# fp16 high and low halves for the later bounds, weight transfers each held behind keys, and constant rows written later, in a chunk-selecting attention with a feed-forward block

## The chip, the core and the metric

The kernel runs on one core of one Trainium2 chip. The metric is the device time of one execution in microseconds (us), lower is better. The core has a matrix engine (TensorE, PE in the profile; its weight loads are listed as PEld), a vector engine (VectorE, DVE), an activation engine (ScalarE, ACT), a general engine (GpSimd, POOL) and a queue engine (SyncE, SP) that here only starts transfers. Each works through its own list of instructions in order; semaphores tie them together.

## What is computed

Attention on 4 images x 8 heads x 768 positions of 64 values, in which each query sees only 6 of 24 chunks of 32 keys; then layer norm and a two-layer feed-forward block with a residual.

```python
k_min = np.min(k_chunks, axis=3)
k_max = np.max(k_chunks, axis=3)
ub = np.sum(np.maximum(q[:, :, :, None, :] * k_min[:, :, None, :, :],
                       q[:, :, :, None, :] * k_max[:, :, None, :, :]), axis=-1)
ub = np.where(causal, ub, -1000000000.0)
top_chunks = np.argsort(ub, axis=-1)[..., -top_k:]
scores = scale * np.matmul(q, k.transpose(0, 1, 3, 2))
mask = sel & (pos[:, None] >= pos[None, :])
...
x = attn_out.transpose(0, 2, 1, 3).reshape(B, S, H * D)
xn = (x - mu) / np.sqrt(var + 1e-06) * g_ln
ch = np.maximum(xn @ w_ch1, 0.0) @ w_ch2
return (x + ch).astype(np.float32)
```

The feed-forward sizes are 512 to 2048 to 512. Inputs and output are fp32.

## The kernel before

The work on attention is cut into 16 batches g of two heads each (4 per image, `HP = 4`). A batch holds the 768 positions as six tiles of 128. Its steps, each a small function:

- `load_qk` (line 166) starts the transfers of q and k on SP's queue, two per tensor, one for each head. For the first batch of the second image (g = 4) a one-element copy on POOL (line 171) from the fourth batch's maxima is written into the tile first, so that the transfer waits for it. `load_v` (line 177) starts v on POOL's queue, which casts to fp16.
- `prep_q` and `prep_k` (lines 196 and 209) transpose q and k on PE (line 193, fp32) into PSUM tiles `tr`, of which there are two. ACT copies q out as fp32 (201); DVE takes minimum and maximum of k over each chunk (217, 218); ACT writes k as fp16 into the rings KA and KB (219, 220). `prep_q2` writes the positive part r of q in fp32 (205) and q times 128 as fp16 into the rings QA and QB (206, 207). `prep_b` makes the fp32 matrix BD of minimum and range, with zeros for the other head (224, 225).
- `bounds` (line 230): one matmul puts the causal mask, -1e30 or 0, into a PSUM tile `sm` (233), then for five query tiles q x minimum and r x range are added to it, ten fp32 products (240). `select` (246) takes the largest eight of 24 bounds per query and head on DVE (251), ten times, and compares all with the seventh (252). `mask_t` (257) transposes the result on PE (261) and DVE puts it into the free rows of QA and QB (262, 263). The rings KA and KB hold constant rows, -61440 for the keys of a chunk, so that the score matmul masks in the same pass.
- `scores` (291): matmuls of line 303 into PSUM tiles `mm`, exponentials on ACT (309) into `pt`. `diag` (314): POOL zeroes the causal triangle (316). `values` (321): matmuls of line 329 into `sm`. `normalise` (334): two DVE operations (339, 340).

After the four batches of an image come layer norm (`stats`, lines 361 to 363; `x_t`, lines 379 to 386) and the feed-forward (`mlp1`, lines 398 and 402; `mlp2`, lines 411, 418 and 422), 64 and 96 pieces for an image.

The order is written by hand: `at(t, function, ...)` puts a piece at a place t, and all pieces are emitted in the order of t (lines 425 to 474). A batch g has its place T = g - 4, and 1.5 more from the second image on; the feed-forward pieces of image b are spread over the places of the batches of image b + 1. Behind this the framework's scheduler, which works on modelled times, gives each engine its list: it takes the piece with the earliest place among those whose operands it deems ready. So an instruction that depends on nothing unfinished can come out ahead of others with earlier places.

`consts_first` (line 99) writes the constants at the start. For five rings (`NK = 5`) it clears parts of QA and QB (123, 124) and copies the constant rows into KA and KB (126, 127) on DVE.

The weights come as eight transfers on POOL's queue, four row blocks of the first matrix (`w1_load`, line 148) at places -1.79 to -1.76 and four of the second (`w2_load`, line 151) at -0.79 to -0.76. In front of either four stands one `w_gate` (line 142):

```python
def w_gate(w, g):
    nc.gpsimd.tensor_copy(w[0:1, 0, 0:1], st[g]["kc"][0:1, 0, 0:1])
```

It writes one element of the first block from the reduced keys of batch 2 (first matrix) or 3 (second matrix). The other three blocks of a matrix share no element with it.

Of the kernel before, what the change touches and what calls it, by code (L numbers as in the profile page):

```python
# [9 lines left out]
ACTF = mybir.ActivationFunctionType  # L10
ALU = mybir.AluOpType
AX = mybir.AxisListType

F32 = mybir.dt.float32
# [5 lines left out]
def kernel(  # L20
# [13 lines left out]
    nc = tc.nc  # L34
# [18 lines left out]
    QS = 128.0  # L53
    HS = 64.0
# [22 lines left out]
    def at(t, fn, *args):  # L77
        pieces.append((t, len(pieces), fn, args))
# [5 lines left out]
    causb = const.tile([P, NT - 1, 2, NCH], BF16, name="causb", tag="causb")  # L84
    RT = const.tile([P, S], F16, name="RT", tag="RT")
# [9 lines left out]
    BD = [ring.tile([P, 2, 2, NCH], F32, name=f"BD{i}", tag=f"BD{i}") for i in range(NB)]  # L95
    NM = 3
    MN = [ring.tile([P, NT - 1, P], F16, name=f"MN{i}", tag=f"MN{i}") for i in range(NM)]

    def consts_first():
# [16 lines left out]
        nc.vector.memset(hsel[0:64, 1:2], 1.0)  # L116
        nc.vector.memset(hsel[64:P, 0:1], 1.0)
# [4 lines left out]
        for i in range(NK):  # L122
            nc.vector.memset(QA[i][64:P, 0:P], 0.0)
            nc.vector.memset(QB[i][0:64, 0:P], 0.0)
        for i in range(NK):
            nc.vector.tensor_copy(KA[i][64:P, :], RT[0:64, :])
            nc.vector.tensor_copy(KB[i][0:64, :], RT[0:64, :])
# [13 lines left out]

    def w_gate(w, g):
        nc.gpsimd.tensor_copy(w[0:1, 0, 0:1], st[g]["kc"][0:1, 0, 0:1])

# [3 lines left out]
    def w1_load(kt):  # L148
        nc.gpsimd.dma_start(w1b[:, kt, :], w1_r[:, kt, :])

    def w2_load(j):
        nc.gpsimd.dma_start(w2b[:, 4 * j:4 * j + 4, :], w2_r[:, 4 * j:4 * j + 4, :])
# [42 lines left out]

    def prep_q(g, t0, t1):
        if t0 == 0:
            for nm in ("q32", "r32"):
                st[g][nm] = prp.tile([P, S], F32, name=nm, tag=nm)
        pst = turn(g, "qn", t0, t1)  # L200
        nc.scalar.copy(st[g]["q32"][:, t0 * P:t1 * P], pst)  # L201

    def prep_q2(g):
        q32, r32 = st[g]["q32"], st[g]["r32"]
        nc.vector.tensor_scalar_max(r32[:, P:], q32[:, P:], 0.0)  # L205
        nc.vector.tensor_scalar(QA[g % NK][0:64, :], q32[0:64, :], QS, None, op0=ALU.mult)
        nc.vector.tensor_scalar(QB[g % NK][64:P, :], q32[64:P, :], QS, None, op0=ALU.mult)

# [20 lines left out]

    def bounds(g):  # L230
        p, bd = st[g], BD[g % NB]
        ub = ps_s.tile([P, NT - 1, 2, NCH], F32, name="sm", tag="sm")
        nc.tensor.matmul(
            ub.rearrange("p s h c -> p (s h c)"), ident_b, causb.rearrange("p s h c -> p (s h c)"),
            start=True, stop=False,
        )
        for s in range(1, NT):
            o = ub[:, s - 1].rearrange("p h c -> p (h c)")
            for nm, arr in (("q32", 0), ("r32", 1)):
                nc.tensor.matmul(  # L240
                    o, p[nm][:, s * P:(s + 1) * P], bd[:, arr].rearrange("p h c -> p (h c)"),
                    start=False, stop=(s == NT - 1 and arr == 1),
                )
        p["ub"] = ub

    def select(g, i):
        ub, mn = st[g]["ub"], MN[i % NM]
        m8 = st[g]["m8"] = smp.tile([P, NT - 1, 2, 8], F32, name="m8", tag="m8")
        for s in range(NT - 1):
            for hh in range(2):  # L250
                nc.vector.max(m8[:, s, hh, :], ub[:, s, hh, :])  # L251
# [198 lines left out]
    at(-1.8, w_gate, w1b, 2)  # L450
    at(-0.8, w_gate, w2b, 3)
    for kt in range(KT1):
        at(-1.79 + 0.01 * kt, w1_load, kt)
        at(-0.79 + 0.01 * kt, w2_load, kt)
# [50 lines left out]
```

## Time and profile before

| what | us |
|---|---|
| median of 3 runs | 355.3 |
| lowest and highest run | 354.95, 359.83 |
| the profiled execution, its own time | 356.89 |
| span of the profiled execution, first to last instruction | 355.2 |

The profile follows one execution. An instruction has its engine, the line of the kernel that made it, its start and length. Matmuls are pipelined and their ends are modelled, so consecutive ones overlap in the list, and the distance from start to start tells the pace. "Idle before, <-" names what the engine last waited for. The granted clock of TensorE is given as a share of its full 2.4 GHz.

### The profile page before, as it was taken

The numbers are of one execution on the slowest core, as the hardware profiler recorded it, in microseconds if no ns is written. First come the engines' busy times: TensorE is split into PE (matmuls) and PEld (weight loads), VectorE is DVE, ScalarE is ACT, GpSimd is POOL, SyncE is SP. The second block draws the span as 40 slices with busy tenths as digits, with TensorE's granted clock in tenths as the row PEclk, the third lists the DMA queues.
The fourth block names the chain that finished last, engine by engine and source line by source line (L and its number), as shares of the span: only waits on it lengthen the run. The fifth ranks groups of instructions, "written<-read, shape, count | busy, mean of one in ns | idle before, by whom it ended". The sixth has DMA issues, their size and how long they took to land.

```text
span 355.2 us, 6715 instructions
## 1 busy us (share of the span) xinstructions
PE 318.4 (90%) x2720; PEld 219.8 (62%) x2720; DVE 183.2 (52%) x573; ACT 181.0 (51%) x261; POOL 73.3 (21%) x108
## 2 busy tenths in 40 slices
PE   3588398799999999999999999998999989899994
PEld 2477377567867667576677657576767545566441
DVE  8767145686245583998171556977170426610021
ACT  2427256776677463627676635428585533166100
POOL 9823304420104223132030303002010100000000
PEclk9999668999999999999999999999999999999999
DMA  9999976993035374363060314100000011100021
GB/s 165 183 203 184 191 104 93 203 152 89 21 71 66 77 127 67 105 97 85 8 97 17 24 59 54 59 31 2 0 2 2 30 45 46 45 18 2 30 80 68
DMA packets 81967, 26.65 MB, mean 75 GB/s; under 512 B 76304, under 2 KB 78352, under 8 KB 81936
## 3 DMA queue, kind: packets, MB, share of 16 engines
q1 hardware_dynamic: 53632, 18.88, 22.8%
q0 software_dynamic: 27776, 7.34, 20.3%
q8 instruction: 21, 0.34, 0.4%
q10 hardware_dynamic: 528, 0.00, 0.1%
q14 instruction: 10, 0.08, 0.1%
HBM read 27.27 MB, written 6.29 MB: 94 GB/s over the span
## 4 chain that ended last, share of the span: by engine, by line
PE 65%; ACT 14%; SPq 6%; DVE 6%; DMA 5%; issue 2%; POOL 0%; ACTq 0%
PE mm L398 20%; PE mm L411 20%; PE sm L240 9%; SPq L173 6%; PE mm L303 6%; ACT pt L309 5%; DMA kn<-in_k_dram 5%; PE sm L329 4%; PE tr L193 4%; ACT hT L402 4%; ACT KB L220 2%; ACT KA L219 2%; DVE ot L418 1%; PE trh L379 1%; DVE r L205 1%
## 5 line engine op out<-in xcount | busy, mean ns | idle before, releaser
L309 ACT ACTIVATE pt<-mm 128x1024 f16<-128x1024 f32 x96 | 86.9, 915 | 61.9 <-PE mm L303 58.9
L398 PE MATMUL mm<-xT,w1b 128*128 128x384 f16 x512 | 93.3, 326 | 5.4 <-ACT hT L402 4.9
L411 PE MATMUL mm<-w2b,hT 128*128 128x512 f16 x384 | 92.7, 379 | 2.1 <-DVE ot L418 1.5
L402 ACT ACTIVATE hT<-mm 128x768 f16<-128x768 f32 x64 | 51.8, 810 | 46.0 <-PE mm L398 45.6
L398 PEld LDWEIGHTS <-w1b 128*128 128x128 f16 x512 | 49.4, 99 | 33.2 <-issue 6.8
L411 PEld LDWEIGHTS <-hT 128*128 128x128 f16 x384 | 36.8, 98 | 36.6 <-issue 3.1
L316 POOL TENSOR_SCALAR_AFFINE_SELECT pt<-pt 128x768 f16<-128x768 f16 x32 | 28.1, 877 | 134.2 <-ACT pt L309 134.2
L418 DVE SCALAR_TENSOR_TENSOR ot<-mm,rstd,x_all 128x512 f32<-128x512 f32 x24 | 17.9, 746 | 49.4 <-PE mm L411 46.7
L303 PE MATMUL mm<-QA,KA 128*128 128x128 f16 (+2 forms) x224 | 37.4, 258 | 4.7 <-ACT pt L309 4.5
L339 DVE RECIPROCAL rden<-sm 128x6 f32<-128x6 f32 x32 | 6.2, 192 | 61.1 <-PE sm L329 60.9
L303 PE MATMUL mm<-QB,KB 128*128 128x128 f16 (+2 forms) x224 | 36.7, 258 | 0.0
L329 PE MATMUL sm<-va,pt 128*128 128x65 f16 x672 | 33.0, 195 | 1.6 <-ACT pt L309 1.1
L329 PEld LDWEIGHTS <-pt 128*128 128x128 f16 x672 | 29.0, 99 | 8.7 <-ACT pt L309 2.3
L240 PE MATMUL sm<-BD,q 128*128 128x48 f32 x160 | 32.7, 289 | 0.8 <-DVE BD L225 0.8
L240 PE MATMUL sm<-BD,r 128*128 128x48 f32 x160 | 33.3, 292 | 0.0
L251 DVE MAX8 m<-sm 128x8 f32<-128x24 f32 x160 | 16.5, 175 | 27.9 <-PE sm L240 23.8
L240 PEld LDWEIGHTS sm<-BD,q 128*128 128x128 f32 x160 | 26.8, 210 | 3.0 <-DVE BD L225 2.7
L184 POOL DMA_DIRECT2D va<-in_v_dram x32 | 27.9, 873 | 0.9
L240 PEld LDWEIGHTS sm<-BD,r 128*128 128x128 f32 x160 | 26.7, 210 | 0.2
L201 ACT COPY q<-tr 128x512 f32<-128x512 f32 (+1 forms) x32 | 15.4, 480 | 21.8 <-PE tr L193 21.7
L193 PE MATMUL tr<-ident_f,qn 128*128 128x128 f32 x96 | 18.5, 305 | 8.3 <-DMA qn<-in_q_dram 4.9
L193 PE MATMUL tr<-ident_f,kn 128*128 128x128 f32 x96 | 18.9, 309 | 7.1 <-DMA kn<-in_k_dram 6.4
(61 smaller groups left out, 313.6 us busy)
## 6 DMA issues: line engine op xcount, KB each, us to landing
qn<-in_q_dram SPq DMA_DIRECT2D x32, 192.0 KB, 3.4
kn<-in_k_dram SPq DMA_DIRECT2D x32, 192.0 KB, 3.9
out_dram<-ot SPq DMA_DIRECT2D x24, 256.0 KB, 2.0
va<-in_v_dram POOLq DMA_DIRECT2D x32, 96.0 KB, 4.2
w1b<-in_moe_w_ch_dram POOLq DMA_DIRECT2D x4, 512.0 KB, 13.4
w2b<-in_moe_w_ch_dram POOLq DMA_DIRECT2D x4, 512.0 KB, 16.4
gstr<-in_moe_g_ln_dram ACTq DMA_DIRECT2D x1, 2.0 KB, 3.2
```

The costliest lines, as they stand in the source:

```text
L173: nc.sync.dma_start(st[g][nm][:, :, hh, :], src[b, 2 * hp + hh].rearrange("(t p) d -> p t d", p=P),)
L184: nc.gpsimd.dma_start(va[:, hh, t0:t1, 0:D], v[b, 2 * hp + hh, t0 * P:t1 * P, :].rearrange("(t p) d -> p t d", p=P),)
L193: nc.tensor.transpose(pst[:, (t - t0) * P:(t - t0 + 1) * P], src[:, t, :, :], ident_f)
L240: nc.tensor.matmul(o, p[nm][:, s * P:(s + 1) * P], bd[:, arr].rearrange("p h c -> p (h c)"), start=False, stop=(s == NT - 1 and arr == 1),)
L303: nc.tensor.matmul(sc[:, hh, o:o + w * P], ks[:, t * P:(t + 1) * P], qs[:, s * P:(s + w) * P], start=True, stop=True,)
L309: nc.scalar.activation(pt[:, n0:n1].rearrange("p n h x -> p h n x"), sc[:, :, 0:o].rearrange("p h (n x) -> p h n x", x=P), ACTF.Exp, scale ...
L316: nc.gpsimd.affine_select(out=dv, in_=dv, compare_op=ALU.is_ge, fill=0.0, base=0, pattern=[[0, 2 * TR], [1, P]], channel_multiplier=-1,)
L329: nc.tensor.matmul(pv[:, hh, s2, :], pt[:, where[t, s], hh, :], va[:, hh, t, 0:D + 1], start=(t == 0), stop=(t == s),)
L398: nc.tensor.matmul(hp_[:, i, 0:TR * P], w1b[:, kt, (m + i) * P:(m + i + 1) * P], xT[:, kt, c], start=(kt == 0), stop=(kt == KT1 - 1),)
L402: nc.scalar.activation(hts[b][:, m:m + 2, c], hp_[:, :, 0:TR * P], ACTF.Relu, scale=HS)
L411: nc.tensor.matmul(yp, hts[b][:, kt, s * P:(s + 1) * P], w2b[:, kt, :], start=(kt == 0), stop=(kt == KT2 - 1),)
L418: nc.vector.scalar_tensor_tensor(ot, yp, rs[b]["rstd"][:, s:s + 1], x_all[:, s].rearrange("p h d -> p (h d)"), op0=ALU.mult, op1=ALU.add,)
```

## The change

For the batches of the second to fourth image (`g >= HP`), the bounds are computed from fp16 pairs. ACT writes the transposed q times 128 as fp16 (`qh`), and DVE writes the rest, q times 128 minus `qh`, as fp16 (`ql`). The positive part is made of both halves (`rh`, `rl`). The matrix BD, now with 128 (`KS`) in place of 1, is split into two fp16 halves as well (`BH`), side by side. The ten fp32 products become twenty fp16 products with 96 output columns: each of `qh`, `ql`, `rh`, `rl` against both halves of the key bounds. The two halves of the result, and the causal mask from a new fp32 table `causf`, are added by DVE in `select`; the mask matmul is gone for these batches. QA and QB are copied from `qh`. The first image's batches keep the fp32 form.

`w_gate` is gone. Each of the eight transfers has its own one-element copy into its own block, from batch 2 for the first matrix and batch 3 for the second. The places move from -1.79 to -2.2 and from -0.79 to -1.2.

The constant rows of rings 0 and 1 are written at the start as before, those of rings 2, 3 and 4 at places -3.7, -3.4 and -3.1.

```diff
@@ -51,6 +51,7 @@
     LN_EPS = 1e-6
 
     QS = 128.0
+    KS = 128.0
     HS = 64.0
     NEGM = 61440.0
     CAUSAL = -1.0e30
@@ -82,6 +83,7 @@
     ident_h = const.tile([P, P], F16, name="ident_h", tag="ident_h")
     ident_b = const.tile([P, P], BF16, name="ident_b", tag="ident_b")
     causb = const.tile([P, NT - 1, 2, NCH], BF16, name="causb", tag="causb")
+    causf = const.tile([P, NT - 1, 2, NCH], F32, name="causf", tag="causf")
     RT = const.tile([P, S], F16, name="RT", tag="RT")
     hsel = const.tile([P, 2], F32, name="hsel", tag="hsel")
     mhalf = const.tile([P, NT], F32, name="mhalf", tag="mhalf")
@@ -93,8 +95,15 @@
 
     NB = 3
     BD = [ring.tile([P, 2, 2, NCH], F32, name=f"BD{i}", tag=f"BD{i}") for i in range(NB)]
+    BH = [ring.tile([P, 2, 2, 2, NCH], F16, name=f"BH{i}", tag=f"BH{i}") for i in range(NB)]
     NM = 3
     MN = [ring.tile([P, NT - 1, P], F16, name=f"MN{i}", tag=f"MN{i}") for i in range(NM)]
+
+    def ring_init(i):
+        nc.vector.memset(QA[i][64:P, 0:P], 0.0)
+        nc.vector.memset(QB[i][0:64, 0:P], 0.0)
+        nc.vector.tensor_copy(KA[i][64:P, :], RT[0:64, :])
+        nc.vector.tensor_copy(KB[i][0:64, :], RT[0:64, :])
 
     def consts_first():
         rr = RT[0:64, :]
@@ -113,18 +122,19 @@
             out=causb, in_=causb, compare_op=ALU.is_ge, fill=CAUSAL,
             base=P, pattern=[[P, NT - 1], [0, 2], [-CH, NCH]], channel_multiplier=1,
         )
-        nc.vector.memset(hsel[0:64, 1:2], 1.0)
-        nc.vector.memset(hsel[64:P, 0:1], 1.0)
+        nc.gpsimd.memset(causf, 0.0)
+        nc.gpsimd.affine_select(
+            out=causf, in_=causf, compare_op=ALU.is_ge, fill=CAUSAL,
+            base=P, pattern=[[P, NT - 1], [0, 2], [-CH, NCH]], channel_multiplier=1,
+        )
+        nc.vector.memset(hsel[0:64, 1:2], KS)
+        nc.vector.memset(hsel[64:P, 0:1], KS)
         nc.vector.memset(hsel[0:64, 0:1], 0.0)
         nc.vector.memset(hsel[64:P, 1:2], 0.0)
         for i in range(NM):
             nc.vector.memset(MN[i], 0.0)
-        for i in range(NK):
-            nc.vector.memset(QA[i][64:P, 0:P], 0.0)
-            nc.vector.memset(QB[i][0:64, 0:P], 0.0)
-        for i in range(NK):
-            nc.vector.tensor_copy(KA[i][64:P, :], RT[0:64, :])
-            nc.vector.tensor_copy(KB[i][0:64, :], RT[0:64, :])
+        for i in range(2):
+            ring_init(i)
         nc.vector.tensor_copy(ident_h, ident_f)
         nc.vector.tensor_copy(ident_b, ident_f)
 
@@ -138,17 +148,16 @@
     w1_r = moe_w_ch1.rearrange("(kt p) n -> p kt n", p=P)
     w2_r = moe_w_ch2.rearrange("(kt p) n -> p kt n", p=P)
 
-
-    def w_gate(w, g):
-        nc.gpsimd.tensor_copy(w[0:1, 0, 0:1], st[g]["kc"][0:1, 0, 0:1])
-
     def g_load():
         nc.scalar.dma_start(gstr, moe_g_ln.rearrange("(kt p) -> p kt", p=P))
 
-    def w1_load(kt):
+
+    def w1_load(kt, g):
+        nc.gpsimd.tensor_copy(w1b[0:1, kt, 0:1], st[g]["kc"][0:1, 0, 0:1])
         nc.gpsimd.dma_start(w1b[:, kt, :], w1_r[:, kt, :])
 
-    def w2_load(j):
+    def w2_load(j, g):
+        nc.gpsimd.tensor_copy(w2b[0:1, 4 * j, 0:1], st[g]["kc"][0:1, 0, 0:1])
         nc.gpsimd.dma_start(w2b[:, 4 * j:4 * j + 4, :], w2_r[:, 4 * j:4 * j + 4, :])
 
 
@@ -193,18 +202,43 @@
             nc.tensor.transpose(pst[:, (t - t0) * P:(t - t0 + 1) * P], src[:, t, :, :], ident_f)
         return pst[:, 0:(t1 - t0) * P]
 
+
+
     def prep_q(g, t0, t1):
+        whole = g < HP
         if t0 == 0:
-            for nm in ("q32", "r32"):
-                st[g][nm] = prp.tile([P, S], F32, name=nm, tag=nm)
+            if whole:
+                for nm in ("q32", "r32"):
+                    st[g][nm] = prp.tile([P, S], F32, name=nm, tag=nm)
+            else:
+                for nm, tag in (("q", "q32"), ("r", "r32")):
+                    t2 = prp.tile([P, 2, S], F16, name=nm + "2", tag=tag)
+                    st[g][nm + "h"], st[g][nm + "l"] = t2[:, 0], t2[:, 1]
         pst = turn(g, "qn", t0, t1)
-        nc.scalar.copy(st[g]["q32"][:, t0 * P:t1 * P], pst)
+        c = slice(t0 * P, t1 * P)
+        if whole:
+            nc.scalar.copy(st[g]["q32"][:, c], pst)
+            return
+        qh, ql = st[g]["qh"], st[g]["ql"]
+        u0 = max(t0, 1) * P
+        u = slice(u0, t1 * P)
+        nc.scalar.activation(qh[:, c], pst, ACTF.Copy, scale=QS)
+        nc.vector.scalar_tensor_tensor(
+            ql[:, u], pst[:, u0 - t0 * P:], QS, qh[:, u], op0=ALU.mult, op1=ALU.subtract,
+        )
 
     def prep_q2(g):
-        q32, r32 = st[g]["q32"], st[g]["r32"]
-        nc.vector.tensor_scalar_max(r32[:, P:], q32[:, P:], 0.0)
-        nc.vector.tensor_scalar(QA[g % NK][0:64, :], q32[0:64, :], QS, None, op0=ALU.mult)
-        nc.vector.tensor_scalar(QB[g % NK][64:P, :], q32[64:P, :], QS, None, op0=ALU.mult)
+        if g < HP:
+            q32, r32 = st[g]["q32"], st[g]["r32"]
+            nc.vector.tensor_scalar_max(r32[:, P:], q32[:, P:], 0.0)
+            nc.vector.tensor_scalar(QA[g % NK][0:64, :], q32[0:64, :], QS, None, op0=ALU.mult)
+            nc.vector.tensor_scalar(QB[g % NK][64:P, :], q32[64:P, :], QS, None, op0=ALU.mult)
+            return
+        qh, ql, rh, rl = (st[g][nm][:, P:] for nm in ("qh", "ql", "rh", "rl"))
+        nc.vector.tensor_scalar_max(rh, qh, 0.0)
+        nc.vector.scalar_tensor_tensor(rl, qh, 0.0, ql, op0=ALU.is_gt, op1=ALU.mult)
+        nc.vector.tensor_copy(QA[g % NK][0:64, :], st[g]["qh"][0:64, :])
+        nc.vector.tensor_copy(QB[g % NK][64:P, :], st[g]["qh"][64:P, :])
 
     def prep_k(g, t0, t1):
         pst = turn(g, "kn", t0, t1)
@@ -227,25 +261,47 @@
             hsel.unsqueeze(1).unsqueeze(3).to_broadcast([P, 2, 2, NCH]), ALU.mult,
         )
 
+        if g >= HP:
+            bh = BH[g % NB]
+            nc.vector.tensor_copy(bh[:, :, 0], bd)
+            nc.vector.tensor_tensor(bh[:, :, 1], bd, bh[:, :, 0], ALU.subtract)
+
     def bounds(g):
         p, bd = st[g], BD[g % NB]
-        ub = ps_s.tile([P, NT - 1, 2, NCH], F32, name="sm", tag="sm")
-        nc.tensor.matmul(
-            ub.rearrange("p s h c -> p (s h c)"), ident_b, causb.rearrange("p s h c -> p (s h c)"),
-            start=True, stop=False,
-        )
-        for s in range(1, NT):
-            o = ub[:, s - 1].rearrange("p h c -> p (h c)")
-            for nm, arr in (("q32", 0), ("r32", 1)):
-                nc.tensor.matmul(
-                    o, p[nm][:, s * P:(s + 1) * P], bd[:, arr].rearrange("p h c -> p (h c)"),
-                    start=False, stop=(s == NT - 1 and arr == 1),
-                )
+        if g < HP:
+            ub = ps_s.tile([P, NT - 1, 2, NCH], F32, name="ub", tag="sm")
+            nc.tensor.matmul(
+                ub.rearrange("p s h c -> p (s h c)"), ident_b, causb.rearrange("p s h c -> p (s h c)"),
+                start=True, stop=False,
+            )
+            for s in range(1, NT):
+                o = ub[:, s - 1].rearrange("p h c -> p (h c)")
+                for nm, arr in (("q32", 0), ("r32", 1)):
+                    nc.tensor.matmul(
+                        o, p[nm][:, s * P:(s + 1) * P], bd[:, arr].rearrange("p h c -> p (h c)"),
+                        start=False, stop=(s == NT - 1 and arr == 1),
+                    )
+        else:
+            bh = BH[g % NB]
+            ub = ps_s.tile([P, NT - 1, 2, 2, NCH], F32, name="ub2", tag="sm")
+            for s in range(1, NT):
+                o = ub[:, s - 1].rearrange("p l h c -> p (l h c)")
+                for i, (nm, arr) in enumerate((("qh", 0), ("ql", 0), ("rh", 1), ("rl", 1))):
+                    nc.tensor.matmul(
+                        o, p[nm][:, s * P:(s + 1) * P], bh[:, arr].rearrange("p l h c -> p (l h c)"),
+                        start=(i == 0), stop=(i == 3),
+                    )
         p["ub"] = ub
 
     def select(g, i):
         ub, mn = st[g]["ub"], MN[i % NM]
         m8 = st[g]["m8"] = smp.tile([P, NT - 1, 2, 8], F32, name="m8", tag="m8")
+        if g >= HP:
+            ubt = smp.tile([P, NT - 1, 2, NCH], F32, name="ubt", tag="ubt")
+            ubm = smp.tile([P, NT - 1, 2, NCH], F32, name="ubm", tag="ubm")
+            nc.vector.tensor_tensor(ubt, ub[:, :, 1], causf, ALU.add)
+            nc.vector.tensor_tensor(ubm, ub[:, :, 0], ubt, ALU.add)
+            ub = ubm
         for s in range(NT - 1):
             for hh in range(2):
                 nc.vector.max(m8[:, s, hh, :], ub[:, s, hh, :])
@@ -447,11 +503,11 @@
             at(t + 0.12, values, g, r)
             at(t + 0.14, normalise, g, r)
     at(-5.5, consts_late)
-    at(-1.8, w_gate, w1b, 2)
-    at(-0.8, w_gate, w2b, 3)
     for kt in range(KT1):
-        at(-1.79 + 0.01 * kt, w1_load, kt)
-        at(-0.79 + 0.01 * kt, w2_load, kt)
+        at(-2.2 + 0.01 * kt, w1_load, kt, 2)
+        at(-1.2 + 0.01 * kt, w2_load, kt, 3)
+    for i in range(2, NK):
+        at(-4.3 + 0.3 * i, ring_init, i)
     for b in range(B):
         e = 4.0 * b + (GAP if b > 0 else 0.0)
         for r in range(NR):
```

## Rows read from the trace of the kernel before

**Rows 1.** The page, part 1: busy us (share of span) xinstructions.

```profile
PE 318.4 (90%) x2720; PEld 219.8 (62%) x2720; DVE 183.2 (52%) x573; ACT 181.0 (51%) x261; POOL 73.3 (21%) x108
```

**Rows 2.** PE's timeline, start: start us, us, what [idle before <- releaser].

```profile
6.69 1.09 PE L193 MATMUL tr<-ident_f,kn 128*128 128x128 f32 x4 [0.71 <-DMA kn<-in_k_dram]
...
12.52 1.11 PE L193 MATMUL tr<-ident_f,qn 128*128 128x128 f32 x4 [2.76 <-ACT KB L220]
...
41.08 1.09 PE L193 MATMUL tr<-ident_f,kn 128*128 128x128 f32 x4 [5.71 <-DMA kn<-in_k_dram]
...
70.38 0.65 PE L398 MATMUL mm<-xT,w1b 128*128 128x384 f16 x3
```

**Rows 3.** Stretches: length, busy PE, PEld, DVE, ACT, POOL; clock, DMA share, GB/s.

```profile
0.00:41.00 41.00, 23.18 (x173) 19.51 (x173) 26.43 (x86) 16.71 (x28) 22.34 (x41) 0.96 1.32 186
41.00:70.40 29.40, 25.47 (x273) 21.21 (x274) 15.43 (x57) 16.89 (x22) 9.67 (x17) 0.77 0.94 135
70.40:310.50 240.10, 230.08 (x2064) 158.57 (x2062) 135.34 (x421) 135.19 (x196) 40.12 (x51) 1.00 0.28 55
```

**Rows 4.** Waits in 70.4:310.5: us in total, times, longest.

```profile
PE mm L398 <- ACT hT L402: 4.9, 14, 1.0
...
PEld L379 <- DVE xc L363: 3.7, 9, 1.2
```

**Rows 5.** DVE in order of time, start, columns as in group 2.

```profile
7.28 0.35 DVE L126 COPY KA<-RT 64x768 f16<-64x768 f16 x1
...
10.00 0.67 DVE L217 TENSOR_REDUCE kc<-tr 128x16 f32<-128x512 f32 x1
```

**Rows 6.** SP's queue in order of time, columns as in group 2.

```profile
16.21 10.56 SPq L173 DMA_DIRECT2D kn<-in_k_dram  x2
```

**Rows 7.** Chain that ended last: start us, us, what.

```profile
24.34 16.49 DMA kn<-in_k_dram
...
42.16 4.13 PE sm L240 x20
...
155.50 2.22 PE sm L240 x20
...
175.70 0.85 PE sm L329 x28
```

**Rows 8.** POOL in order of time, start, columns as in group 2.

```profile
11.57 1.12 POOL L149 DMA_DIRECT2D w1b<-in_moe_w_ch_dram  x2
...
26.35 0.76 POOL L152 DMA_DIRECT2D w2b<-in_moe_w_ch_dram  x1
...
28.53 0.18 POOL L143 CAST w1b<-kc 1x1 f16<-1x1 f32 x1
29.00 0.56 POOL L149 DMA_DIRECT2D w1b<-in_moe_w_ch_dram  x1 [0.30 <-POOL w1b L143]
...
42.96 0.18 POOL L143 CAST w2b<-kc 1x1 f16<-1x1 f32 x1 [5.24 <-DVE kc L217]
```

**Rows 9.** PE in order of time, later, columns as in group 2.

```profile
177.69 0.39 PE L303 MATMUL mm<-QA,KA 128*128 128x128 f16 x4
177.91 0.39 PE L303 MATMUL mm<-QB,KB 128*128 128x128 f16 x4
```

**Rows 10.** The page, part 5: busy us, mean ns | idle before.

```profile
L329 PEld LDWEIGHTS <-pt 128*128 128x128 f16 x672 | 29.0, 99 | 8.7 <-ACT pt L309 2.3
```

**Rows 11.** DVE by line, 70.4:310.5: busy us, mean ns | idle before.

```profile
L340 DVE TENSOR_TENSOR x_all<-sm,rden 128x384 f16<-128x384 f32 x25 | 13.9, 557 | 0.8
...
L418 DVE SCALAR_TENSOR_TENSOR ot<-mm,rstd,x_all 128x512 f32<-128x512 f32 x18 | 13.4, 745 | 14.3 <-PE mm L411 11.6 <-issue 2.6
...
L205 DVE TENSOR_SCALAR r<-q 128x640 f32<-128x640 f32 x12 | 7.0, 585 | 4.5 <-ACT q L201 4.5
...
L252 DVE TENSOR_TENSOR MN<-sm,m 128x240 f16<-128x240 f32 x12 | 4.8, 399 | 0.1
...
L225 DVE TENSOR_TENSOR BD<-kc,hsel 128x96 f32<-128x96 f32 x12 | 3.1, 258 | 0.4
```

## The prediction, made before the changed kernel was run

> **What bounds the kernel now.** I read the page's engine shares first: TensorE (PE) is busy 90% of the span, VectorE (DVE) 52%, ScalarE (ACT) 51%, GpSimd (POOL) 21% [rows 1]. That average hides two different programs, so I cut the span where the feed-forward part begins, at the first matmul of line 398, 70.38 us [rows 2], and where the last attention work ends, 310.5 us [rows 3].
>
> In the middle, 70.4 to 310.5 us, PE is busy 230.1 of 240.1 us at a granted clock of 1.00, which is the 2.4 GHz level. DVE and ACT are busy 135 us each, 56% [rows 3]. The twelve later attention batches (one batch is two heads) run there, interleaved with the feed-forward of the first three images. The list of waits shows PE held back by others for few microseconds: the largest are 4.9 us for ACT's line 402, and 3.7 us of weight loading behind DVE's line 363 [rows 4]. What takes PE time out of this stretch shortens it, as long as no other engine becomes the bound.
>
> The first 70.4 us are the opposite. PE is busy 23 of 41 us and then 25 of 29 us, the latter at a mean clock of 0.77 [rows 3]: the lower level for nearly half of that stretch. The four first batches run alone as a chain of short steps. Three things in it are late. (1) PE's transposes of the second batch wait 2.76 us for ACT's copy of the first batch's keys [rows 2]. That copy comes behind DVE's minimum and maximum of the same PSUM tile, which begin at 10.00 us behind the constant rows of all five rings [rows 5], though the keys were transposed by 6.69 + 1.09 = 7.8 us [rows 2]. (2) PE waits 5.71 us for the fourth batch's keys, until 41.08 us [rows 2]. The transfers' queue is slow to take them: from 16.21 us two issues last 10.56 us [rows 6], and in the chain 16.49 us follow in which the keys are under way [rows 7]. (3) After that wait PE runs at the low clock: the bounds of the next batch take 4.13 us where a later one takes 2.22 us [rows 7].
>
> The transfers collide with the weights. In the code the first weight transfer stands behind a one-element copy from the third batch's keys, yet the trace shows six of the eight weight transfers issued between 11.57 and 26.35 us, ahead of both copies (28.53 and 42.96 us) [rows 8]. Only the slice that the copy writes really waits for it; the other slices don't depend on it and were put into gaps. A slice is 128 x 2048 values of fp16, 0.52 MB; six are 3.1 MB, of 186 GB/s x 41 us = 7.6 MB moved in that stretch [rows 3].
>
> **The change, part by part.**
>
> *Constant rows later.* Three rings' rows leave the head of DVE's queue. The last three pairs of copies run from 7.28 us to the first reduction at 10.00 us [rows 5], so the reduction can begin when the keys are there, at 7.8 us: 2.2 us earlier for the chain behind it. The copies return later, 2.7 us of them, beside batches two and three, where DVE is busy only 26 of 41 us [rows 3]; without that cover they cost at most what they save. Bounds: 0 to 2.7 us gained; I take 2.2. The new fp32 causal table adds two POOL operations ahead of the first loads' end; I book nothing, since two or three early weight issues leave the same queue.
>
> *Weight transfers behind keys.* Every slice is now written by its own one-element copy, so all eight transfers are really held: four until the third batch's keys are reduced, four until the fourth's. The fourth batch's keys then share the engines with no weights: 7.6 - 3.1 = 4.5 MB at 186 GB/s end by some 24 us (an estimate from [rows 3]) rather than 41. PE's order is fixed and it came to these keys at 41.08 - 5.71 = 35.4 us, so the gain is that wait, 5.7 us, and not 17. The low clock follows the idle time, so the bounds behind it should run as elsewhere: 4.13 - 2.22 = 1.9 us [rows 7]. Bounds for both: 0 (another wait takes its place) to 17 us (the whole chain moves up with the keys). I take 7.6.
>
> The new waits stand in POOL's queue, and behind them stand the diagonal masks (line 316) that the value matmuls need, the v loads, and the copies of line 171 that release the second image's loads on SP. One guarded slice costs from 28.53 to 29.00 + 0.56 = 1.0 us of POOL [rows 8], and there are six more guards of some 0.5 us. POOL is busy 9.7 of 29.4 us there [rows 3]; I book 0.5 us lost, bounds 0 to 8. Arrival of the weights: four slices are 2.1 MB, 11 us at 186 GB/s, from about 28 us on; the first use is at 70.4 - 9 = 61 us, so they are in time.
>
> *Bounds in fp16.* Now a batch has ten fp32 products that PE runs as 20 matmuls in 2.22 us, 111 ns each [rows 7]. They become 20 fp16 matmuls of 96 columns. Nearest rows: 28 fp16 matmuls of 65 columns in 0.85 us, 30 ns each [rows 7], and four of 128 columns from 177.69 to 177.91 us, 55 ns each [rows 9]. Between them 96 columns give 42 ns (bounds 30 and 55), 0.85 us. The mask matmul of 240 columns goes too: 240/128 x 55 = 0.10 us. Per batch 2.22 - 0.85 + 0.10 = 1.47 us, for twelve batches 17.6 us (14.5 to 20.6).
>
> What speaks against so much: each of the 20 brings its own weight load, and a weight load of 128 fp16 columns lasts 99 ns by itself [rows 10]. In these rows it is hidden, since the matmuls start 55 and 30 ns apart. The Trainium skill (TensorE: Matmul & The Clock Gate, Back-to-back issue gap) gives about 81 ns per matmul for a sustained stream of weight loads and matmuls of 128 columns; this trace, with its 55 ns, does not agree. By that figure 20 would cost 1.62 us, the twelve batches would gain 8.4 us, and the sum would be 342.6 us.
>
> *What DVE gets for it.* Per later batch: the low half of q, a two-input operation from PSUM over 384 and 256 columns: by 0.557 us for 384 and 0.399 us for 240 [rows 11], 1.0 us. The low half of the positive part, 640 columns, two fp16 inputs: between the one-input row of 0.585 us and the pace of line 418 (0.745 us for 512, so 0.93); I take 0.75. Two small operations on the key bounds at 0.258 us: 0.5. Two additions of 240 columns from PSUM at 0.399 us: 0.8. The replaced operations I book as equal. Sum 3.0 us per batch, 36 us for twelve, all in the middle stretch: DVE goes from 135 to 171 us of some 227, from 56% to 75%. ACT keeps its count. This work is off PE's path only while DVE has idle time when PE needs it. PE's largest wait on DVE now is 3.7 us [rows 4]; if it grows as busy over idle time does (0.56/0.44 to 0.75/0.25, 2.35 times), that is 8.7, so 5.0 us lost. Bounds 0 and all 36.
>
> *Sum*, against the profiled execution, 356.9 us (span 355.2 and 1.7 around it; 1.6 over the median of 355.3): start -2.2 - 7.6 + 0.5 = -9.3; middle -17.6 + 5.0 = -12.6; together -21.9, so 335.0 there and 333.4 beside the median.
>
> **The rivals.**
>
> *A. DVE becomes the bound of the middle* (this one can end on the other side). Place: the PSUM tile of the transposed queries is now read by ACT and then DVE before PE may fill it again, and the sums before the maxima queue behind layer-norm bursts. For it: 75% busy, in order, with every step of a batch passing through it. Against: the waits on it are small now, and the list gives half a batch period between bounds and mask. If PE waits x us more per batch, the time is 355.3 - 9.3 - 17.6 + 12x. At x = 1.47 the middle gains nothing (346); from x = 2.24 it is slower than before, from 2.83 by over 2%; at all 3.0 it is 364. Chance of x over 1.47: 0.18, of which 0.10 under 1.7, 0.05 up to 2.83, 0.03 above.
>
> *B. The start doesn't move*: POOL's guarded transfers hold the masks, or the sequence of short steps is as long without the keys' wait, since ACT has its own queue of exponentials there. For it: POOL waited 5.24 us for the same keys [rows 8]. Against: PE's idle 5.71 us are plainly a transfer's. Time 355.3 - 12.6 = 342.7. Chance 0.14.
>
> *C. The start moves as far as the keys do*, 41 to 24 us: the order is laid out anew and the clock stays up. For it: 0.77 mean clock. Against: ACT and DVE still have 17 and 15 us of work after 41 us [rows 3]. Time 355.3 - 17 - 12.6 = 325.7. Chance 0.12.
>
> *D. The weight loads of the fp16 matmuls are not hidden.* Then the matmuls start 99 ns apart [rows 10], 20 take 1.98 us, a batch gains 0.24 + 0.10 us, twelve 4.1. For it: 96 columns of one PSUM bank are summed four times in a row, which neither near row does. Against: the 30 and 55 ns. Time 355.3 - 9.3 - 4.1 + 5.0 = 346.9. Chance 0.04. The Trainium skill's page on TensorE, named above, would put the time between this and the forecast.
>
> **How the numbers follow.** My forecast has the rest, 0.52, with 327 to 340 as its own range (DVE's loss 0 to 10, the start some 1.5 us either way). Over all cases 8 in 10 lie between 321 (C, with 4 us of the remaining low clock back) and 346 (B, D and A up to where the middle gains nothing). About 2% is what a measurement of this kernel can tell from no change, so 348.2 and 362.4 are the borders. Faster: 0.52 + 0.12 + 0.14 + 0.04 and A's 0.10, less a little of B and D, 0.90. Same 0.07, slower 0.03.
>
> **What would show it.** In the changed profile: no weight transfer ahead of the third batch's keys; no wait of PE for a key transfer near 35 us; the first reduction near 8 us; line 398 beginning near 61 us; bounds of a later batch in 0.85 us; DVE near 75% in the middle; PE's waits on DVE below 10 us. I am wrong if line 398 still begins near 70 us, if PE's waits on DVE exceed 18 us, or if the 20 matmuls take over 1.3 us.

## The result, and the profile after

The changed kernel takes 331.69 us (median of 4 runs, 330.16 to 333.07), the kernel before 355.12 us beside it. The ratio is 0.934, with a 95% interval of 0.929 to 0.939. The prediction was 333.4 us, 321 to 346.

The page, part 1, after: PE has lost 17 us of busy time against [rows 1], DVE has gained 21.

```profile
PE 301.0 (91%) x2708; PEld 199.2 (60%) x2708; DVE 203.9 (62%) x657; ACT 180.1 (54%) x261; POOL 74.0 (22%) x116
```

PE's timeline after, the lines that answer to [rows 2] and the bounds of the first later batch (line 290):

```profile
6.87 1.09 PE L202 MATMUL tr<-ident_f,kn 128*128 128x128 f32 x4 [0.71 <-DMA kn<-in_k_dram]
...
10.54 1.12 PE L202 MATMUL tr<-ident_f,qn 128*128 128x128 f32 x4 [0.60 <-ACT KB L254]
...
33.95 0.66 PE L202 MATMUL tr<-ident_f,kn 128*128 128x128 f32 x4
...
60.54 0.65 PE L454 MATMUL mm<-xT,w1b 128*128 128x384 f16 x3
...
70.39 0.24 PE L290 MATMUL ub<-BH,q 128*128 128x96 f16 x2
...
71.15 0.25 PE L290 MATMUL ub<-BH,r 128*128 128x96 f16 x2
71.24 0.51 PE L202 MATMUL tr<-ident_f,kn 128*128 128x128 f32 x3
```

The wait for the fourth batch's keys is gone (33.95 us, no idle time). The feed-forward begins at 60.54 instead of 70.38 us. Twenty fp16 matmuls start between 70.39 and 71.24 us: 0.85 us, where [rows 7] had 2.22.

The transfers, POOL's timeline after, to be held against [rows 8]: no weight goes out before its keys.

```profile
26.58 0.54 POOL L156 CAST w1b<-kc 1x1 f16<-1x1 f32 x4
27.05 2.18 POOL L157 DMA_DIRECT2D w1b<-in_moe_w_ch_dram  x4
...
35.84 0.54 POOL L160 CAST w2b<-kc 1x1 f16<-1x1 f32 x4
```

Stretches from here on go from the first feed-forward matmul to the last batch's value matmuls, 28 in a row, at 304.8 us before and 280.4 after. Columns are those of [rows 3]; first the kernel before, then after:

```profile
70.40:304.80 234.40, 225.34 (x2012) 155.52 (x2010) 130.99 (x408) 134.38 (x195) 39.94 (x50) 1.00 0.29 56
```

```profile
60.50:280.40 219.90, 211.36 (x2000) 138.25 (x1998) 153.18 (x492) 133.72 (x195) 39.89 (x50) 1.00 0.32 62
```

So of the 24.4 us that the span lost (355.2 to 330.8), 9.8 came from the start and 14.5 from the middle; the rest of the feed-forward, some 50 us, is unchanged. DVE is busy 70% of the middle (153.2 of 219.9), not 75.

### The profile page after: what moved, and what is told of

It is laid out like the page before. It is cut to its first block, busy times and chain, and to the rows that moved or that the text cites. A ratio compares the mean times of both kernels' runs of the same rounds, so it can differ in the third digit from the quotient of the medians.

```text
span 330.8 us, 6794 instructions
## 1 busy us (share of the span) xinstructions
PE 301.0 (91%) x2708; PEld 199.2 (60%) x2708; DVE 203.9 (62%) x657; ACT 180.1 (54%) x261; POOL 74.0 (22%) x116
## 4 chain that ended last, share of the span: by engine, by line
PE 60%; ACT 19%; DVE 15%; issue 2%; DMA 1%; SPq 0%; POOL 0%; ACTq 0%
PE mm L454 20%; PE mm L467 18%; ACT pt L365 8%; PE mm L359 6%; ACT hT L458 5%; PE sm L385 4%; PE ub L280 4%; PE tr L202 3%; ACT KB L254 3%; ACT KA L253 2%; DVE ot L474 2%; PE ub L290 2%; DVE kc L251 2%; DVE kc L252 2%; PE trh L435 2%
## 5 line engine op out<-in xcount | busy, mean ns | idle before, releaser
L359 PE MATMUL mm<-QA,KA 128*128 128x128 f16 (+2 forms) x224 | 35.9, 251 | 5.2 <-ACT pt L365 4.3
L359 PE MATMUL mm<-QB,KB 128*128 128x128 f16 (+2 forms) x224 | 35.4, 252 | 0.0
L253 ACT CAST KA<-tr 64x512 f16<-64x512 f32 (+1 forms) x32 | 15.0, 468 | 17.3 <-DVE kc L252 17.2
L359 PEld LDWEIGHTS <-KA 128*128 128x128 f16 x224 | 19.0, 102 | 8.9 <-issue 2.3
L359 PEld LDWEIGHTS <-KB 128*128 128x128 f16 x224 | 18.6, 101 | 6.7 <-issue 4.2
L202 PE MATMUL tr<-ident_f,kn 128*128 128x128 f32 x96 | 19.7, 306 | 1.6 <-DMA kn<-in_k_dram 0.7
L251 DVE TENSOR_REDUCE kc<-tr 128x16 f32<-128x512 f32 (+1 forms) x32 | 17.7, 552 | 3.1 <-PE tr L202 2.9
L396 DVE TENSOR_TENSOR x_all<-sm,rden 128x384 f16<-128x384 f32 x32 | 17.7, 555 | 0.8
L226 DVE SCALAR_TENSOR_TENSOR q<-tr,q 128x384 f16<-128x384 f32 (+1 forms) x24 | 11.7, 488 | 9.9 <-ACT q L225 9.6
```

The source lines that it names most:

```text
L202: nc.tensor.transpose(pst[:, (t - t0) * P:(t - t0 + 1) * P], src[:, t, :, :], ident_f)
L251: nc.vector.tensor_reduce(kc[:, 0, n], view, axis=AX.X, op=ALU.min)
L253: nc.scalar.copy(KA[g % NK][0:64, c], pst[0:64, :])
L359: nc.tensor.matmul(sc[:, hh, o:o + w * P], ks[:, t * P:(t + 1) * P], qs[:, s * P:(s + w) * P], start=True, stop=True,)
```

## The experiments

Every run has its two lengths from PE's timeline: the place of the first feed-forward matmul ("start") and the distance from there to the last 28 value matmuls ("middle"). The medians come from the timed runs.

| kernel | start, us | middle, us | median, us |
|---|---|---|---|
| before | 70.4 | 234.4 | 355.1 to 355.9 |
| after | 60.5 | 219.9 | 331.7 |
| e1 all but the fp16 bounds | 58.3 | 234.4 | 344.8 |
| e2 the fp16 bounds alone | 60.8 | 220.7 | 333.8 |
| e3 the guards alone | 62.7 | 234.4 | 348.2 |
| e4 the later rings alone | 72.4 | 234.4 | 355.5 |
| e10 an unread table alone | 60.5 | 234.4 | 347.9 |
| e9 after, guards at the first batch's keys | 66.8 | 219.9 | 338.0 |
| e11 after, rings early | 59.7 | 220.9 | 332.5 |
| e7 after, fp16 in all batches | 67.5 | 219.9 | 339.1 |
| e12 after, fp16 from the third batch | 64.0 | 219.9 | 335.9 |
| e5 after, DVE +2.4 us per batch | 58.5 | 229.2 | 340.9 |
| e6 after, DVE +4.9 us per batch | 61.5 | 241.6 | 353.9 |
| e8 after, one DVE operation on POOL | 58.6 | 232.3 | 343.0 |

### The parts alone

**e1: the guards and the later rings, with fp32 bounds in all batches.** The table is still written, though the sum no longer reads it.

```diff
+    FB = B * HP
...
-        whole = g < HP
+        whole = g < FB
...
-        if g >= HP:
+        if g >= FB:
```

> The change without its fp16 bounds: all sixteen batches keep the fp32 bounds; guarded weights and later constant rows stay. My theory (start and middle are separate gains): line of the first feed-forward matmul at 60.5 us as in the changed kernel, the middle as long as before (236 us), so about 345 us, 9 to 10 under the kernel before. Rival B (the start gains only because of something in the new order of the fp16 kernel): first feed-forward matmul near 70 us, about 355 us.

Measured 344.75 us (344.67 to 347.06), ratio 0.973 (0.969 to 0.977). The middle has exactly its old length, so start and middle are separate gains of this change, as expected. The start is 2 us shorter than that of the changed kernel (58.3 against 60.5 us), though the first four batches are the same; "What stays open" comes back to that.

**e2: the fp16 bounds alone.**

```diff
-    for kt in range(KT1):
-        at(-2.2 + 0.01 * kt, w1_load, kt, 2)
-        at(-1.2 + 0.01 * kt, w2_load, kt, 3)
-    for i in range(2, NK):
-        at(-4.3 + 0.3 * i, ring_init, i)
+    at(-1.8, w_gate, w1b, 2)
+    at(-0.8, w_gate, w2b, 3)
+    ...
```

> The fp16 bounds alone; weights and constant rows as before. My theory: the start unchanged, first feed-forward matmul near 70 us, the middle shorter by 14 to 15 us, about 340.5 us. If the middle's gain needed the new start, less than 10 us would be gained, over 345 us.

Measured 333.78 us (333.28 to 334.31), ratio 0.941 (0.938 to 0.944). That is 6.7 us better than expected and nearly the whole gain. The middle did as expected (220.7). The miss is the start: it is at 60.8 us although six weight transfers still go out early, from 12.20 to 27.90 us. The two single parts add up to 31.7 us, more than the change's 23.4, so some 8 us of the start are counted twice.

**e3 and e4: the guards alone, the rings alone.**

> The kernel before with each of the eight weight transfers behind its own guard and at its new place; constant rows and bounds as before. My theory: PE's 5.7 us wait for the fourth batch's keys is gone and the clock stays up behind it, so 7 to 8 us gained, about 347.5 us; the first reduction stays at 10 us. Rival B: another wait takes its place, within 2 us of before.

> The kernel before with the constant rows of three rings later; weights and bounds as before. By the step in my prediction taken alone: 2.2 us gained. But if the fourth batch's keys, which land at 40.8 us whatever DVE does, set the end of the start stage, the gain is swallowed by the wait for them: PE comes to them 2 us earlier and waits 2 us longer, so 0 gained, about 355 us. I expect the second: within 1 us of before.

e3: 348.23 us (346.63 to 349.42), ratio 0.981 (0.977 to 0.986), start at 62.7 us: 6.9 us gained, close to what I expected. e4: 355.51 us, ratio 1.003 (1.000 to 1.006): nothing, as expected, but not in the way that I expected. Its profiled execution took 358.9 us, 3.4 more than its median, so its start of 72.4 us may be long by some of that. PE's timeline of e4 has a wait for the third batch's keys, and the wait of [rows 2] with a later end:

```profile
26.75 0.63 PE L195 MATMUL tr<-ident_f,kn 128*128 128x128 f32 x4 [1.99 <-DMA kn<-in_k_dram]
...
43.02 1.09 PE L195 MATMUL tr<-ident_f,kn 128*128 128x128 f32 x4 [5.49 <-DMA kn<-in_k_dram]
```

PE did not come to the fourth batch's keys 2 us earlier and wait 2 us longer. It came at 43.02 - 5.49 = 37.5 us, later than the 35.4 us of before, and waited about as long. The keys themselves landed 2 us later, so their landing is not fixed, though I had taken it to be.

### Why the fp16 bounds alone moved the start

e2 adds two operations to POOL ahead of its first v transfers: the fp32 causal table. I made the kernel before with these two and nothing else; nothing reads the table.

```diff
+        nc.gpsimd.memset(causf, 0.0)
+        nc.gpsimd.affine_select(
+            out=causf, in_=causf, compare_op=ALU.is_ge, fill=CAUSAL, ...
+        )
```

> The kernel before plus the two GpSimd operations that write the fp32 causal table, which nothing reads. Theory T (found behind the fp16-only run): these 0.8 us hold GpSimd's first v transfers back, so SyncE hands over the fourth batch's keys before its queue fills up, and they land 5 us earlier; then this kernel alone begins the feed-forward near 61 to 63 us and takes about 347 us. Rival: the start of the fp16-only kernel came from its other work; then this kernel is the kernel before, 355 us with the feed-forward at 70 us.

Measured 347.92 us (346.17 to 349.00), ratio 0.973 (0.965 to 0.981), start at 60.5 us. An idle table gains 7.6 us, about what the guards alone gain (6.9; the intervals overlap). SP's queue and POOL's timeline of e10:

```profile
13.43 10.42 SPq L179 DMA_DIRECT2D kn<-in_k_dram  x2
```

```profile
3.78 0.29 POOL L117 MEMSET causf<- 128x240 f32 x1
...
4.45 0.50 POOL L118 TENSOR_SCALAR_AFFINE_SELECT causf<-causf 128x240 f32<-128x240 f32 x1
...
4.98 1.94 POOL L190 DMA_DIRECT2D va<-in_v_dram  x2
...
17.12 0.75 POOL L158 DMA_DIRECT2D w2b<-in_moe_w_ch_dram  x1 [0.37 <-DMA va<-in_v_dram]
25.62 0.76 POOL L158 DMA_DIRECT2D w2b<-in_moe_w_ch_dram  x1
```

POOL's timeline of the kernel before at the same places:

```profile
3.87 1.01 POOL L184 DMA_DIRECT2D va<-in_v_dram  x1
...
16.33 0.75 POOL L152 DMA_DIRECT2D w2b<-in_moe_w_ch_dram  x1 [0.66 <-DMA va<-in_v_dram]
18.15 0.74 POOL L152 DMA_DIRECT2D w2b<-in_moe_w_ch_dram  x1 [1.07 <-DMA va<-in_v_dram]
```

POOL's first v transfer leaves at 4.98 us; before, it left at 3.87. SP hands over the fourth batch's keys from 13.43 us, where [rows 6] has 16.21. The queue stalls at these keys as before, for two issues of 10.4 us together, but 2.8 us earlier; theory T had them handed over ahead of the stall. One weight transfer fewer is ahead of them, too: the fifth leaves at 25.62 us instead of 18.15. The second of the two issues starts at 19.98 us and lands 15.4 us later, at 35.4 us; before, the keys landed at 24.34 + 16.49 = 40.8 us [rows 7]. PE's timeline of e10 shows the transposes of these keys at 35.66 us, with 1.47 us of waiting, instead of 41.08:

```profile
35.66 0.63 PE L199 MATMUL tr<-ident_f,kn 128*128 128x128 f32 x4 [1.47 <-DVE x_all L346]
```

That the two operations do it is shown. That it goes by the later v transfers, by the order in which the queues fill or by the weight transfer that leaves later is only read from these rows; no run moved one of them alone, and only one length of POOL work was tried.

**e9: the guards' time.** All eight guards of the changed kernel wait for the first batch's keys, so they open early.

```diff
-        at(-2.2 + 0.01 * kt, w1_load, kt, 2)
-        at(-1.2 + 0.01 * kt, w2_load, kt, 3)
+        at(-2.2 + 0.01 * kt, w1_load, kt, 0)
+        at(-1.2 + 0.01 * kt, w2_load, kt, 0)
```

> The changed kernel with its eight guards, but all behind the first batch's keys (ready near 9 us) instead of the third's and fourth's. Every guard stays, only its time moves. If the contention of weights with queries and keys is what cost the start, eight transfers of 4.2 MB go out from about 14 us, the fourth batch's keys land at 40 us or later, and the gain of the start is lost: 340 to 343 us. If the guard's place doesn't matter, 332 us.

Measured 338.00 us (336.56 to 338.80), 2 us under the expected band; the start at 66.8 us. The first transfers went out from 12.79 us, and PE's timeline has the wait for the keys back, though they landed at 37 us and not at 40 or later:

```profile
37.39 1.08 PE L202 MATMUL tr<-ident_f,kn 128*128 128x128 f32 x4 [4.46 <-DMA kn<-in_k_dram]
```

So even with the table in place, 6.3 of the 9.8 us hang on when the weights leave. Guard and table are two remedies for one wait.

**e11: the rings in the changed kernel.** `ring_init` runs for all five rings in `consts_first`.

> The changed kernel with the constant rows of all five rings written at the start again; guards and fp16 bounds stay. By the step of my prediction: with the keys' wait gone, the first reduction comes 1.3 to 2.2 us later and so does everything behind it, 333 to 334 us. Rival: some wait further on absorbs it, as it did when this part was made alone, 331.7 us.

Measured 332.47 us (331.52 to 335.06) over six runs, ratio 0.937 (0.932 to 0.941) against 0.934 (0.929 to 0.939) for the changed kernel. In its trace the first reduction comes at 9.23 us instead of 8.00, yet the feed-forward begins at 59.7 us. At the fourth batch's keys e11 is about 1 us behind e5 (34.23 against 33.37 us), whose first four batches are those of the changed kernel. By the medians, 0.8 us apart, the rings are not told from nothing, and neither expectation is confirmed.

### What VectorE costs in the middle

**e5 and e6: more DVE work.** The low half of the positive part is computed four times (e5) or seven (e6, with `range(6)`).

```diff
         nc.vector.scalar_tensor_tensor(rl, qh, 0.0, ql, op0=ALU.is_gt, op1=ALU.mult)
+        for _ in range(3):
+            nc.vector.scalar_tensor_tensor(rl, qh, 0.0, ql, op0=ALU.is_gt, op1=ALU.mult)
```

> The changed kernel with the low half of the positive part computed four times instead of once: 3 x 0.81 = 2.4 us more VectorE work in each of twelve batches, 29 us in all, nothing else. My theory (VectorE has slack): VectorE goes from 70% to about 83% of the middle and PE loses 3 to 6 us, 335 to 338 us. Rival A (VectorE is already the bound of the middle): most of the 29 us show, over 350 us.

> The same with seven times instead of one: 4.9 us more per batch, 58 us in all; VectorE would need 216 of the middle's 222 us. My theory: here VectorE becomes the bound, 350 to 365 us, and the second 29 us cost far more than the first. Rival A: the second step costs as much as the first, over 375 us.

Measured 340.85 us (339.50 to 342.07) and 353.88 us (350.04 to 355.55), ratios 0.954 (0.946 to 0.962) and 0.994 (0.990 to 0.999). The stretches of the middle, e5 and e6, columns as in [rows 3]:

```profile
58.50:287.80 229.30, 214.93 (x2001) 139.19 (x1999) 179.08 (x528) 134.26 (x195) 41.05 (x50) 0.99 0.33 62
```

```profile
61.50:303.10 241.60, 217.34 (x1999) 139.73 (x1997) 205.04 (x564) 134.33 (x195) 40.23 (x50) 0.98 0.30 56
```

DVE is not the bound that rival A made it: of the first 26 us of added busy time 9.3 show in the middle, of the next 26 us 12.4. But it is not free either, and e5 cost more than I expected (9 us, not 3 to 6). The time of e6 lies in my range by luck: DVE did not become the bound, it is busy 85% of the middle, and the second step cost a third more than the first, not far more. The price of a DVE microsecond in this stretch is 0.36 in the first step and 0.48 in the second, at 78 and 85% busy. Part of that price is the clock: it is granted at 0.99 and 0.98 in these stretches, against 1.00 in the changed kernel's, since some 3 us of e5's middle and 8 us of e6's run at the lower level. At half the pace that is, by estimate, up to 1.7 and 4 us. Between the two steps, some 37 us more DVE work (3 us per batch) would have eaten the middle's gain.

**e8: one DVE operation on POOL.**

```diff
-        nc.vector.scalar_tensor_tensor(rl, qh, 0.0, ql, op0=ALU.is_gt, op1=ALU.mult)
+        nc.gpsimd.tensor_scalar(rl, qh, 0.0, None, op0=ALU.is_gt)
+        nc.gpsimd.tensor_tensor(rl, rl, ql, ALU.mult)
```

> The changed kernel with the low half of the positive part on GpSimd, as a comparison and a product, in place of one VectorE operation of 0.81 us per later batch: 9.7 us less for VectorE. By the slope of the added VectorE work (29 us more cost 9 us) this should give 1 to 3 us, 329 to 331 us. Rival: GpSimd's two operations come later than VectorE's one and hold the bounds or the diagonal masks, 332 to 336 us.

Measured 342.98 us (341.53 to 343.84), ratio 0.962 (0.956 to 0.968): 11 us slower than the changed kernel, far outside both expectations. DVE's groups by line in the middle, first the changed kernel, then e8:

```profile
L241 DVE COPY QB<-q 64x768 f16<-64x768 f16 x12 | 4.6, 385 | 0.2
...
L238 DVE TENSOR_SCALAR r<-q 128x640 f16<-128x640 f16 x12 | 3.9, 321 | 0.0
```

```profile
L238 DVE TENSOR_SCALAR r<-q 128x640 f16<-128x640 f16 x12 | 8.6, 715 | 0.0
L242 DVE COPY QB<-q 64x768 f16<-64x768 f16 x12 | 8.4, 701 | 0.2
```

POOL needs 1.83 and 1.44 us for the two operations, and meanwhile DVE's neighbours on the same tile get slower, in the mean 0.72 for 0.32 us and 0.70 for 0.39 us. The mean hides two cases: most of these operations are as fast as ever, but in most batches one of them lasts until POOL's is done. One batch in DVE's timeline of e8, and the operation of POOL beside it:

```profile
103.90 1.49 DVE L238 TENSOR_SCALAR r<-q 128x640 f16<-128x640 f16 x1
105.32 0.34 DVE L241 COPY QA<-q 64x768 f16<-64x768 f16 x1
```

```profile
103.82 1.40 POOL L240 TENSOR_TENSOR r<-r,q 128x640 f16<-128x640 f16 x1
```

The Trainium skill (SBUF — State Buffer, Who interferes with whom) says that DVE's second pair of SBUF ports is shared with GpSimd, that copies and tensor_scalar operations can run in modes which take both pairs, and that whoever issues first then holds the shared pair for its whole instruction while the other is blocked. The trace agrees with that in these rows. DVE is busy 158.3 us in e8's middle against 153.2, though 9.7 us of work were taken from it. How the 12.4 us by which the middle grew divide between DVE's delay and the later result of POOL, the rival that I had named, is not shown: PE's wait for the split key bounds (BH) grew from 0.7 to 4.6 us, and some 5 us of e8's middle run at the lower clock.

### fp16 in the first image

**e7 and e12: fp16 bounds in all batches, and from the third on** (`g < 0` and `g < 2` in place of `g < HP`).

> The changed kernel with the fp16 bounds in the first image's four batches too. There the chain runs alone: PE gains 1.4 us per batch (2.6 for the first, at the low clock), VectorE gets 2 to 2.5 us more per batch, mostly in the chain from transposes to mask. Theory (in the start the chain counts, not PE's time): no gain, 331 to 336 us. Rival (PE's time counts there too): 4 to 6 us gained, 326 to 328 us.

> The same, but only from the third batch on, so that the first two, whose chain is bare, keep the fp32 bounds. Theory: between the changed kernel and the kernel with all batches in fp16, 330 to 334 us. Rival (PE's time counts): 2 to 3 us gained, 329 us.

Measured 339.12 us (338.16 to 340.90) and 335.86 us (335.16 to 336.22). The middle is the same to 0.1 us; the start grows from 60.5 to 67.5 and 64.0 us, 1.8 us for each batch that is switched. It is worse than either expectation. That a batch's steps form a bare chain here, so that 1.4 us of PE saved do not pay for the 2.4 us that DVE gets, fits the sign, but gives 1.0 us per batch and not 1.8; no run took the steps apart. At the fourth batch's keys e7 is already 3.5 us behind (37.42 against 33.95 us). Behind them the profiled executions also run longer at the lower clock: from 50 to 58 us it is granted at 0.51 in e7 and 0.71 in e12, at 1.00 in the changed kernel. The clock alone does not explain the loss: at one mean granted clock, 0.995, e12 took 335.6 us and the changed kernel 330.9.

## Why the prediction was right, and where its steps were not

**The middle.** The PE term was right: 42 ns per matmul from the rows of 30 and 55 ns, 0.85 us for twenty [rows 7, 9], and 0.85 us were measured. Rival D (99 ns [rows 10]) is out, and so are, for this kernel, the 81 ns of the Trainium skill (TensorE: Matmul & The Clock Gate, Back-to-back issue gap). The sum of 17.6 us shows as 14.5 in the middle, 3.1 us less; I had booked 5.0 us less, for PE waiting on DVE. That the 3.1 us are such waits is not shown. By the two stretches under the result PE's time without work did not grow: 234.40 - 225.34 = 9.1 us before, 219.90 - 211.36 = 8.5 us after. What is missing is missing from PE's busy time, which fell by 14.0 us; as the ends of matmuls are modelled, short waits can count as busy there. The largest wait on DVE now, PE's weight loads in the middle, answers to the second of [rows 4]:

```profile
PEld L435 <- DVE xc L419: 5.1, 12, 1.2
```

I had it grow to 8.7, that is by 5.0 us; it grew by 1.4. The term below it was mis-sized: DVE got 22 us of busy time instead of 36. The added operations cost what [rows 11] gave. Their rows after:

```profile
L239 DVE SCALAR_TENSOR_TENSOR r<-q 128x640 f16<-128x640 f16 x12 | 9.8, 812 | 0.0
...
L226 DVE SCALAR_TENSOR_TENSOR q<-tr,q 128x384 f16<-128x384 f32 x12 | 6.7, 554 | 2.8 <-ACT q L225 2.8
...
L226 DVE SCALAR_TENSOR_TENSOR q<-tr,q 128x256 f16<-128x256 f32 x12 | 5.1, 421 | 7.0 <-ACT q L225 6.8
...
L302 DVE TENSOR_TENSOR ubt<-ub,causf 128x240 f32<-128x240 f32 x12 | 4.8, 403 | 11.3 <-PE ub L290 11.3
L303 DVE TENSOR_TENSOR ubm<-ub,ubt 128x240 f32<-128x240 f32 x12 | 4.8, 403 | 0.2
```

With the two on the key bounds, 0.26 and 0.21 us, that is 3.06 us per batch, where I said 3.0. But the replaced operations, which I booked as equal, became faster with fp16 on both sides: the positive part takes 0.32 us (it was 0.585 [rows 11]), the two copies into QA and QB 0.34 and 0.39 us (0.54 and 0.56 before), 0.64 us per batch. What then remains to the 22 us is mostly overlap of consecutive operations, some 5 us, which each length counts twice.

**The start.** The total was right, 9.3 us foretold and 9.8 found, in part by luck: three of its steps were not, and the 9.8 us are those of one execution (e1, alike in this stretch, has 12.1).

- The keys' wait and the clock behind it were rightly read: 5.71 us of waiting are gone [rows 2]. From the transposes of these keys to the feed-forward 26.6 us pass instead of 29.3, where I had booked 1.9 us for the bounds alone. But much of the start's gain would have come without the guards: I booked nothing for the two POOL operations of the causal table, and e10 shows 7.6 us for them alone. The step that failed is the sentence that early weight issues "leave the same queue": it priced POOL's time and not what POOL's time does to the order in which two queues fill.
- The rings' 2.2 us were added to the keys' wait as if both lay on the path. Alone they give nothing (e4), where PE still waits for the keys, until 43.0 us. In the changed kernel they are not told from nothing (e11).
- The 0.5 us for guards holding POOL cannot be seen in the total.

**The rivals.** A is out as a bound, but its slope is real (e5, e6). B (the start doesn't move) and C (it moves as far as the keys) are out: SP had handed the keys over by 15.35 + 3.51 = 18.9 us, as its queue after shows, and the second issue, at 17.07 us, landed 7.5 us later, at 24.6 us. That is the 24 us of my estimate, but PE came to the keys at 33.95 us, as its fixed order said.

```profile
15.35 3.51 SPq L182 DMA_DIRECT2D kn<-in_k_dram  x2
```

**What stays open.** The start's length differs by some 2 us between kernels that are alike there: 60.5 us after, and 58.3 to 58.6 in e1, e5 and e8, whose first four batches are the same. The granted clock goes with it. The stretch from 46 to 50 us, columns as in [rows 3], after and then e5:

```profile
46.00:50.00 4.00, 4.00 (x36) 3.81 (x36) 1.51 (x13) 1.02 (x1) 1.74 (x4) 0.57 1.24 206
```

```profile
46.00:50.00 4.00, 3.40 (x43) 2.62 (x42) 2.56 (x15) 2.68 (x3) 2.04 (x5) 1.00 1.24 206
```

In the changed kernel's trace some of the fourth batch's bounds, from 46.6 us on, run at the lower clock, as in this row of PE's timeline against 0.39 us for the same two matmuls:

```profile
46.57 0.62 PE L280 MATMUL ub<-BD,r 128*128 128x48 f32 x2
```

Why the clock falls there in one and not in the other was not settled. Every start in the table is that of one execution.

## What to carry to other kernels

Price an edit by the stretch in which it lies: twelve batches in a stretch that PE fills turn PE's time into time, and the same edit in the four batches of a bare chain loses. Two remedies for one wait don't add up, so take each part alone before you credit a part; here a table that nobody reads did what a guard was written for. And before work is moved to an idle engine, look at what it shares with the busy one.

## What the runs showed of the hardware that I had not expected

- 0.8 us of unrelated GpSimd work ahead of its first transfers made the fourth batch's keys arrive 5.4 us earlier (35.4 instead of 40.8 us). SyncE's queue came to its stall, with these keys at its head, 2.8 us sooner, and one weight transfer fewer left before them; which of the two counts is not shown.
- Two operations of 3.3 us on GpSimd slowed the fp16 operations of VectorE beside them: most kept their 0.3 us, but one in most batches lasted until GpSimd was done (1.49 us). Taking 9.7 us off VectorE left it busier by 5 us.
- The middle's length repeats to 0.1 us: 234.4 us in five kernels with fp32 bounds in the later batches and 219.9 us in four with fp16 bounds, whatever the start did (220.7 and 220.9 in e2 and e11, whose middles begin with 2 us at the lower clock, 0.50).
